# Layer A scores: the mask as 64 extra factors of queries and keys, in place of a mask product

## The chip, the cores and the metric

One core of a Trainium2 chip runs the whole program. TensorE multiplies, VectorE and ScalarE evict and transpose, GpSimd copies and issues small transfers, SyncE issues the streamed weights. The metric is the device time of one execution, in microseconds (us); lower is better. In the profile PE is TensorE's products, PEld its weight loads, DVE VectorE, ACT ScalarE, POOL GpSimd, SP SyncE.

## The reference, cut to what matters

Four layers in the order A, B, A, B, each added to its input after a layer norm. Only layer A is touched. It is a recurrence: the 2048 rows are cut into 64 segments of 32 rows, and eight memory rows that go in front of a segment are an output of the segment before it.

```python
L = M + seg_len                      # 8 + 32
mask = (idx[:, None] < M) | (idx[:, None] >= idx[None, :])
mem = mem0
for s in range(n_seg):               # 64 segments, one after the other
    h = concatenate([mem, xs], axis=1)
    q, k, v = einsum of h with Wq, Wk, Wv      # 32 heads of 192
    scores = einsum('bhqe,bhke->bhqk', q, k) * scale
    scores = where(mask, scores, -1e9)
    o = einsum('bhqk,bhke->bhqe', softmax(scores), v)
    o = einsum('bhte,hed->btd', o, Wo)
    mem = o[:, :M, :]
    outs.append(o[:, M:, :])
```

## The kernel before

**Tiling.** A segment's heads are worked in four rounds of eight. In one round the 32 rows that depend on the recurrence (8 memory rows and 24 rows of the segment) are projected on the chain; the last 8 rows of each segment don't depend on it as queries and keys, and a preparation stage (`A_pre`) has computed them for all segments and stored them in DRAM (`kqb_d`, `vb_d`). A score matrix is 80 by 80 for two heads: 2 x 32 columns of chain rows and 16 of prepared rows.

**Eight heads as six chunks.** The projection of queries (or keys) of one round gives 128 partitions by 384 columns in PSUM (`project`): six chunks of 64 columns. A head has 192 features, which is one chunk of 128 and a half. Three chunks hold two heads: chunk 0 is the one head's, chunk 2 the other's, and the middle chunk is shared, its upper 64 partitions one head's rest and its lower 64 the other's. `to_raw` evicts the 384 columns to bf16 (ScalarE), `to_rows` transposes them into `KT` or `QT` (VectorE). For the queries GpSimd then copies the second half of both middle chunks into two chunks of their own (line 1075) and clears it in its old place (line 1076), so that the half that belongs to the other head meets zeros.

**Scores.** `scores` opens the PSUM bank with a mask product: the identity (80 by 80) times a constant mask tile, four times side by side, 320 columns (line 1091). Six products add the scores (line 1098): four of 80 columns, two of 160. `weigh` takes the exponential (ScalarE, line 1181).

**A segment in program order.** `A_chain` is scheduled by hand: each engine runs its instructions in the order in which they are written. Round 0 projects Q, K and V. For n = 0, 1, 2 the steps are: project Q of round n + 1; scores and exponential of round n; `next_kq` puts prepared columns into `KT` and `QT` (GpSimd, line 1036); in round 1 sixteen products with Wo; project K of round n + 1; `attend` round n (lines 1111 and 1118); `tails_after`, a transfer issued by GpSimd that brings 16 prepared value rows into one of two value tiles (`extra_v`, line 1040), read two rounds later and issued when `attend` has read that tile; `fetch_kq` (line 1031); project V of round n + 1; weighing and transposing the outputs. After V of round 3 come the last scores, with steps of the output product around them: `STEPS` says how many ahead of the scores and how many between scores and `attend`. The segment ends with `attend` of round 3, the last twelve output steps, four filling products (`keep_busy`), and the new memory rows (`wt`, `hT`), which the next segment's first Q projection waits for.

**Streamed weights.** Not all weights fit. Per segment SyncE issues seven loads of 384 KB (three Wq, two Wk, two Wv slots, line 705) and four of 320 KB (`wo_rows`, line 750). Each waits for one step on TensorE: every projection releases one load when it is done (`self.release(last)`), in the order Wq, Wq, Wq, Wk, Wk, Wv, Wv, then the four Wo pieces. The Wv slots are read by V of round 3, the Wo pieces by the segment's last steps.

**Stores.** With s > 0, the tail output of the segment before is evicted after K of round 0, transposed and stored after V of round 0 (`store_tail`, line 1156); the rows of the segment before are stored after `fetch_kq` of round 0 (`store_rows`, line 1027). The transfers that GpSimd issues run in the order of its program.

Of the kernel before, what the change touches and what calls it, by code (L numbers as in the profile page):

```python
# [8 lines left out]
P = 128  # L9
BF16 = mybir.dt.bfloat16  # L10
F32 = mybir.dt.float32
# [16 lines left out]

STEPS = (1, 5)

# [4 lines left out]
def ap3(ap, dims):  # L35
    return bass.AP(tensor=ap.tensor, offset=ap.offset, ap=[list(d) for d in dims])
# [86 lines left out]
class Kernel:  # L123
# [508 lines left out]
    def build_A_consts(self):  # L632
        nc, const = self.nc, self.const

        mk = const.tile([P, 80], BF16, name="mask_st")
        nc.gpsimd.memset(mk[:], MASK_NEG)

        def keep(m, base, pattern, mult):  # L640
            nc.gpsimd.affine_select(out=m, in_=m, compare_op=ALU.is_ge, fill=MASK_NEG, base=base, pattern=pattern,
                                    channel_multiplier=mult)

        for G in range(2):
            for c in (slice(32 * G, 32 * G + 32), slice(64 + G, 80, 2)):
                nc.gpsimd.memset(mk[32 * G:32 * G + 32, c], 0.0)
            keep(mk[32 * G:32 * G + 32, 32 * G + 8:32 * G + 32], 8, [[1, 24]], -1)
            for c in (slice(32 * G, 32 * G + 8), slice(64 + G, 80, 2)):
                m = mk[64:80, c]
                nc.gpsimd.memset(m, 0.0)  # L650
                if G == 0:
                    keep(m, 7, [[0, 8]], -1)
                else:
                    keep(m, -8, [[0, 8]], 1)
                if c.start >= 64:
                    keep(m, 8 * G, [[1, 8]], -1)
        self.mk = mk

# [128 lines left out]
    def A_pre(self, xn_dram, li, load_matrix, piece, wo_mid, wo_end, lay_out_wo, early_wo, x_raw):  # L787
# [12 lines left out]
        with ExitStack() as es:  # L800
# [102 lines left out]
            for h, ri, r in steps:  # L903
# [14 lines left out]
                turn += 1  # L918
                if x_raw is not None and h == 0 and ri == 1:
                    self.build_A_consts()  # L920
# [56 lines left out]
    def A_chain(self, xn_dram, at_dram, li, load_slot, piece, late_wo, load_both, wo, low):  # L977
# [3 lines left out]
        with tc.tile_pool(name=f"A{li}_ch", reuse_waits="tile", bufs=1) as sp, \  # L981
                tc.tile_pool(name=f"A{li}_pq", reuse_waits="tile", bufs=2, space=bass.MemoryType.PSUM) as pqp, \
                tc.tile_pool(name=f"A{li}_po", reuse_waits="tile", bufs=1, space=bass.MemoryType.PSUM) as pop, \
                tc.manual_schedule():
            KT = sp.tile([P, 6, 80], BF16, name="KT")
            QT = sp.tile([P, 8, 80], BF16, name="QT")
            Vs = [sp.tile([P, 4 * VH], BF16, name=f"Vp{i}") for i in range(2)]
# [3 lines left out]
            ots = [self.under[:, self.ot_at + 384 * i:self.ot_at + 384 * i + 384] for i in range(2)]  # L991
            for i, t in enumerate((KT, QT, *Vs)):
                (nc.vector if i % 2 else nc.gpsimd).memset(t[:], 0.0 if i < 2 else 1.0)
            xv = xn_dram.rearrange("(s t) d -> t s d", t=32)
# [4 lines left out]
            def rounds(s):  # L999
                return range(NR) if s % 2 == 0 else range(NR - 1, -1, -1)  # L1000
# [33 lines left out]
            def extra_kq(kqb):  # L1034
                for t, c in ((QT, 96), (KT, 0)):
                    nc.gpsimd.tensor_copy(out=t[:, 0:6, 64:80], in_=kqb[:, c:c + 96].rearrange("p (c q) -> p c q", q=16))

# [4 lines left out]
            def project(hT, ps, m, n, s, steps):  # L1042
                order = rounds(s)
                r = order[n]
                ns = SLOTS[m]
                for i in steps:
                    b = (i + KC - ns) % KC if n == 0 else i
                    w = piece(m, r, b)
                    for g in range(4):
                        if m == "V":  # L1050
                            hp = 2 * (g % 2) + g // 2
                            rhs = w[:, 384 * hp:384 * hp + 384]
                        else:
                            w3 = w[:, 32 * g:32 * g + 32]
                            rhs = ap3(w3, [list(w3.ap[0]), [P, 6], [768, 2], [1, 32]])
                        o = ps
                        last = nc.tensor.matmul(o[32 * g:32 * g + 32, 0:384], lhsT=hT[:, b, :], rhs=rhs, start=(i == 0),  # L1057
                                         stop=(i == KC - 1), tile_position=(0, 32 * g), skip_group_check=True)
# [6 lines left out]

            def to_raw(ps, tag):
                raw = sp.tile([P, 384], BF16, name="raw", tag=tag)
                nc.scalar.activation(out=raw[:], in_=ps[:, 0:384], func=ACT.Copy)  # L1068
                return raw

            def to_rows(raw, m):
                t = KT if m == "K" else QT
                nc.vector.transpose(out=t[:, 0:6, 0:64], in_=raw[:, :].rearrange("p (c j) -> p c j", j=64))  # L1073
                if m == "Q":
                    nc.gpsimd.tensor_copy(out=QT[64:P, 6:8, :], in_=QT[64:P, 1:5:3, :])  # L1075
                    nc.gpsimd.memset(QT[64:P, 1:5:3, :], 0.0)  # L1076

# [9 lines left out]
            def scores():  # L1087

                S = pop.tile([P, 512], F32, name="ps_s", tag="s")
                m = self.mk[0:80, :]  # L1090
                nc.tensor.matmul(S[0:80, 0:320], lhsT=self.ident[0:80, 0:80], rhs=ap3(m, [list(m.ap[0]), [0, 4], [1, 80]]),  # L1091
                                 start=True, stop=False, skip_group_check=True)
                for x in range(2):
                    for i, q in ((0, slice(3 * x, 3 * x + 1)), (1, slice(3 * x + 1, 7 + x, 5 - 2 * x)),
                                 (2, slice(3 * x + 2, 3 * x + 3))):
                        c0 = 160 * x + (80 if i == 2 else 0)
                        n = 2 if i == 1 else 1
                        nc.tensor.matmul(S[0:80, c0:c0 + 80 * n], lhsT=KT[:, 3 * x + i, :], rhs=QT[:, q, :],  # L1098
                                         start=False, stop=(x == 1 and i == 2), skip_group_check=True)
                return S  # L1100
# [48 lines left out]

            def turn_tail(rows):  # L1150
                otb = sp.tile([P, 192], BF16, name="otb", tag="otb", bufs=2)
                self.chain_end = [nc.vector.transpose(out=otb[:], in_=rows[:])]  # L1152
                return otb

            def store_tail(otb, s, r):
                nc.gpsimd.dma_start(out=self.otb_d[:, s, 192 * (r // 2):192 * (r // 2) + 192], in_=otb[:])  # L1156

# [52 lines left out]
            for s in range(NSEG):  # L1210
# [3 lines left out]

                def q_or_k(m, n):
                    ps = pqp.tile([P, 512], F32, name="ps_qk", tag="qk")
                    project(hT, ps, m, n, s, range(KC))
                    return to_raw(ps, "rawk" if m == "K" else "raw")

# [14 lines left out]
                raw = q_or_k("K", 0)  # L1234
                to_rows(raw, "K")
                if s > 0:
                    rows = tail_rows(rct, "OTh")
                if s == 0:
# [3 lines left out]
                v_rows(pv, 0, "sv")  # L1242
                if s > 0:
                    store_tail(turn_tail(rows), s - 1, rounds(s - 1)[L])
                OTs = []
# [18 lines left out]
                for n in range(L):  # L1264
                    raw = q_or_k("Q", n + 1)
                    if n == 2:
                        otb = turn_tail(otr)
                    E = weigh()
                    next_kq(s, n)
                    to_rows(raw, "Q")  # L1270
                    if n == 1:
# [17 lines left out]
                    if n == 1:  # L1289
                        rct = weigh_tail()  # L1290
                    to_rows(raw, "K")
                    pv = v_banks()
# [36 lines left out]
                wo_round(W, order[L], OTs[L], False, True)  # L1329
                idle = pqp.tile([P, 512], F32, name="ps_idle", tag="qk")  # L1330
                for _ in range(4):
# [10 lines left out]
                W_done = W  # L1342
            store_tail(turn_tail(tail_rows(rct, "OTh")), NSEG - 1, order[L])
            keep_rows(W_done)
# [83 lines left out]
```

## Time and profile before

| | us |
|---|---|
| median of 3 runs | 3346.97 |
| lowest and highest | 3339.17, 3349.75 |
| the profiled execution, its own time | 3343.23 |
| span of its trace | 3341.5 |
| TensorE, VectorE, ScalarE, GpSimd busy | 3154.1, 2132.4, 1778.2, 1581.9 |
| the mask product, 512 times, mean of one | 0.331 |
| eviction of queries or keys, 1024 times, mean of one | 0.490 |
| transposition of queries, 512 times, mean of one | 0.579 |

A row of a group reads: line, engine, operation, output<-inputs, shape, count | busy time, mean of one in ns | idle time of the engine just before, and what ended it. A row of the timeline or of the chain of waits reads: start in us, length in us, engine, line, operation, xcount. Lengths of products include the pipeline, so the distance between two starts, not the length, is what a product takes from TensorE. A DMA row of the chain of waits runs from the issue to the landing that ended the wait.

### The profile page before, as it was taken

What the parts mean: (1) busy time and instruction counts of PE and PEld (TensorE: products, weight loads), DVE (VectorE), ACT (ScalarE), POOL (GpSimd) and SP (SyncE); (2) the same over time, 40 slices, a digit from 0 to 9 for tenths busy, and PEclk for the clock granted to TensorE, in tenths of its full rate; (3) what the DMA queues carried; (4) which work ended last, traced back from release to release, by engine and by line L of the source; (5) the groups of instructions that cost most, each with busy time, mean ns of one, the idle gap of its engine ahead of it and who ended that gap; (6) DMA issues with size and microseconds to landing.
All of it is one profiled execution on the core that took longest, in us unless ns stands there. A gap on an engine that the chain in (4) does not pass through costs nothing.

```text
span 3341.5 us, 141361 instructions
## 1 busy us (share of the span) xinstructions
PE 3154.1 (94%) x58946; PEld 2007.3 (60%) x59218; DVE 2132.4 (64%) x5569; ACT 1778.2 (53%) x4225; POOL 1581.9 (47%) x3921
## 2 busy tenths in 40 slices
PE   9889999999999999899999899999999999998999
PEld 7656666656666666555367566666666666665553
DVE  5456666666666666646643566666666666666565
ACT  3245555555555565546433455555555555655363
POOL 3345555555555555530123455555555555555300
PEclk9999999999999999999999999999999999999999
DMA  8887777767767777750285767777677776768400
GB/s 308 317 297 235 241 242 238 255 225 249 245 228 254 238 253 240 266 175 1 101 305 194 243 233 250 236 246 248 230 251 239 248 246 233 255 232 284 135 1 32
DMA packets 325241, 747.58 MB, mean 224 GB/s; under 512 B 66066, under 2 KB 100490, under 8 KB 321530
## 3 DMA queue, kind: packets, MB, share of 16 engines
q1 hardware_dynamic: 254586, 638.46, 54.7%
q0 software_dynamic: 67808, 86.77, 8.9%
q10 hardware_dynamic: 2208, 13.30, 1.0%
q8 instruction: 465, 7.62, 0.9%
q14 instruction: 174, 1.43, 0.1%
HBM read 668.78 MB, written 77.00 MB: 223 GB/s over the span
## 4 chain that ended last, share of the span: by engine, by line
PE 55%; DMA 19%; POOL 7%; DVE 6%; issue 5%; ACT 2%; POOLq 0%; SPq 0%; DVEq 0%; ACTq 0%
PE ps_qk L1057 15%; PE ps_w L1163 10%; DMA Vp<-vb 9%; PE ps_v L1057 6%; DMA arena<-in_A_Wv_dram 5%; DMA arena<-wo_rows 4%; PE ps_pre L936 3%; PE kv L1383 2%; DVE wt L1337 2%; PE ps_o L1111 2%; PE ps_s L1098 2%; PE ps_wo L429 2%; PE ps_s L1091 2%; PE ps_pre L963 2%; DVE hT L1339 2%
## 5 line engine op out<-in xcount | busy, mean ns | idle before, releaser
L1057 PE MATMUL ps_qk<-arena,hT 128*32 128x384 bf16 x20480 | 996.1, 327 | 51.9 <-DVE hT L1339 37.9
L1057 PEld LDWEIGHTS <-hT 128*32 128x32 bf16 x30720 | 785.6, 96 | 429.5 <-issue 39.1
L1068 ACT ACTIVATE raw<-ps_qk 128x384 bf16<-128x384 f32 x1024 | 502.0, 490 | 519.7 <-PE ps_qk L1057 515.4
L1057 PE MATMUL ps_v<-arena,hT 128*32 128x384 bf16 x8192 | 432.7, 326 | 10.8 <-DMA arena<-in_A_Wv_dram 9.3
L1136 ACT ACTIVATE osc<-ps_o,rc 128x192 bf16<-128x192 f32 x896 | 334.6, 417 | 140.0 <-DVE rc L1130 129.1
L1073 DVE STREAM_TRANSPOSE QT<-raw 128x384 bf16<-128x384 bf16 x512 | 296.3, 579 | 155.0 <-ACT raw L1068 99.3
L1075 POOL COPY QT<-QT 64x160 bf16<-64x160 bf16 x512 | 163.2, 319 | 487.9 <-DVE QT L1073 472.0
L1040 POOL DMA_DIRECT2D Vp<-vb x512 | 257.6, 503 | 202.1 <-issue 99.1
L1073 DVE STREAM_TRANSPOSE KT<-raw 128x384 bf16<-128x384 bf16 x512 | 295.9, 578 | 78.6 <-ACT raw L1068 62.5
L1085 DVE CAST Vp<-ps_v 64x384 bf16<-64x384 f32 x512 | 286.3, 559 | 50.6 <-ACT Vp L1083 38.5
L1163 PE MATMUL ps_w<-arena,under 128*32 128x320 bf16 x6144 | 304.7, 301 | 2.3 <-issue 1.9
L1031 POOL DMA_DIRECT2D kqb<-kqb x512 | 292.3, 571 | 18.9 <-DMA vb<-arena 1.8
L1083 ACT ACTIVATE Vp<-ps_v 64x384 bf16<-64x384 f32 x512 | 247.9, 484 | 16.6 <-PE ps_v L1057 13.9
L1181 ACT ACTIVATE E<-ps_s 80x320 bf16<-80x320 f32 x512 | 221.4, 432 | 59.4 <-PE ps_s L1098 42.1
L1020 ACT ACTIVATE wh<-ps_w 64x160 f32<-64x160 f32 x256 | 76.6, 299 | 309.8 <-DVE wt L1337 265.8
L1098 PE MATMUL ps_s<-QT,KT 128*80 128x80 bf16 (+1 forms) x3072 | 234.2, 213 | 7.2 <-POOL QT L1076 3.5
L1156 POOL DMA_DIRECT2D otb<-otb x256 | 142.2, 555 | 203.1 <-DVE otb L1152 202.8
L1126 DVE RECIPROCAL rc<-ps_o 128x2 f32<-128x2 f32 x384 | 65.5, 171 | 247.9 <-PE ps_o L1111 247.6
L1098 PEld LDWEIGHTS <-KT 128*80 128x80 bf16 x3072 | 209.9, 119 | 17.8 <-issue 4.2
L936 PEld LDWEIGHTS <-arena 128*128 128x128 bf16 x1920 | 189.1, 99 | 43.7 <-DMA arena<-in_A_Wk_dram 13.2
L1111 PE MATMUL ps_o<-Vp,E 80*32 80x193 bf16 x4096 | 178.7, 248 | 37.6 <-DMA Vp<-vb 31.9
L94 DVE CAST arena<-ps_pre 128x512 bf16<-128x512 f32 (+1 forms) x160 | 102.3, 646 | 144.3 <-PE ps_pre L936 97.1
(161 smaller groups left out, 5115.2 us busy)
## 6 DMA issues: line engine op xcount, KB each, us to landing
arena<-wo_rows SPq DMA_DIRECT2D x560, 320.0 KB, 6.2
arena<-in_A_Wq_dram SPq DMA_DIRECT2D x427, 384.0 KB, 3.8
arena<-in_A_Wk_dram SPq DMA_DIRECT2D x298, 384.0 KB, 5.1
arena<-in_A_Wv_dram SPq DMA_DIRECT2D x290, 384.0 KB, 6.0
kqb<-kqb POOLq DMA_DIRECT2D x512, 48.0 KB, 4.6
vb<-arena POOLq DMA_DIRECT2D x128, 97.0 KB, 5.9
Vp<-vb POOLq DMA_DIRECT2D x512, 24.2 KB, 4.6
kqb<-arena SPq DMA_DIRECT2D x8, 1536.0 KB
```

Source lines behind the costliest of these rows:

```text
L936: nc.tensor.matmul(ps[:, T * i:T * i + T], lhsT=w[b][:, P * c:P * c + P], rhs=xBT[:, b, :], start=(b == 0), stop=(b == KC - 1))
L1031: nc.gpsimd.dma_start(out=kqb[:], in_=self.kqb_d[r, :, s, :])
L1040: nc.gpsimd.dma_start(out=Vs[n % 2][64:80, :], in_=self.vb_d[s, r].rearrange("g t f -> (g t) f"))
L1057: last = nc.tensor.matmul(o[32 * g:32 * g + 32, 0:384], lhsT=hT[:, b, :], rhs=rhs, start=(i == 0), stop=(i == KC - 1), tile_position=(0, 3 ...
L1068: nc.scalar.activation(out=raw[:], in_=ps[:, 0:384], func=ACT.Copy)
L1073: nc.vector.transpose(out=t[:, 0:6, 0:64], in_=raw[:, :].rearrange("p (c j) -> p c j", j=64))
L1083: nc.scalar.activation(out=o, in_=i, func=ACT.Copy)
L1085: nc.vector.tensor_copy(out=o, in_=i)
L1098: nc.tensor.matmul(S[0:80, c0:c0 + 80 * n], lhsT=KT[:, 3 * x + i, :], rhs=QT[:, q, :], start=False, stop=(x == 1 and i == 2), skip_group_c ...
L1111: nc.tensor.matmul(O[G][32 * h:32 * h + 32, VH * G:VH * G + 193], lhsT=E[0:80, 80 * h + 32 * G:80 * h + 32 * G + 32], rhs=V[0:80, VH * h:V ...
L1136: nc.scalar.activation(out=out, in_=i, func=ACT.Copy, scale=rc[G])
L1163: step = nc.tensor.matmul(W[q:q + 32, 0:320], lhsT=OT[i // 6][:, i % 6 // 2, 32 * (i % 2):32 * (i % 2) + 32], rhs=rhs, start=(first and i ...
```

## The change

The middle chunk is now two chunks, each with one half occupied: a round's queries (and keys) take 8 chunks, 512 columns, four for each pair of heads. `project` writes the 384 columns into a PSUM bank with a gap: partitions 0 to 63 leave chunk 3 of each four empty, partitions 64 to 127 chunk 0. Queries and keys have one PSUM bank each, kept for the whole layer (`psq`, `psk`), and the empty halves of these banks hold 64 constant factors, written once per layer: `w` with the queries and `u` with the keys, built so that their product is the mask. Evicting and transposing 512 columns carries them along; the columns of the prepared rows have factors of their own (`wt`, `ut`), written once into `KT` and `QT`. So the mask product goes, the scores become eight products of 80 columns, and the two GpSimd steps on the queries' halves go.

With it come these moves:

- Eviction (ScalarE) and transposition (VectorE) of queries and keys have 512 columns in place of 384. Keys of round 3 are done in two halves of 256.
- The prepared columns go into `KT` and `QT` (now one tile `QK`) with two copies of 64 partitions by 192 elements in place of two of 128 by 96.
- The tail of the segment before is evicted, transposed and stored, and its rows are stored, ahead of the first Q projection's eviction. The rows' store comes first.
- `STEPS` is (2, 5) in place of (1, 5).
- The transposed tails lie in parts of `ots` instead of tiles of their own; the bank for the filling products is the one of the scores.
- The factors are built by GpSimd in the preparation stage of both A layers (24 instructions; the mask tile was built once), and eight small VectorE copies at the start of each chain place them.

```diff
-STEPS = (1, 5)
+STEPS = (2, 5)
...
+            QK = sp.tile([P, 2, 8, 80], BF16, name="QK")
+            KT, QT = QK[:, 0], QK[:, 1]
+            psq, psk = [pqp.tile([P, 512], F32, name=f"ps_qk_{m}") for m in "qk"]
...
+            u, w, ut, wt = self.factors()
+            for ps, part, t, tail in ((psq, w, QT, wt), (psk, u, KT, ut)):
+                for h, c in ((slice(64, P), 0), (slice(0, 64), 3)):
+                    o = ps[h, :].rearrange("p (x c j) -> p x c j", c=4, j=64)[:, :, c, :]
+                    nc.vector.tensor_copy(out=o, in_=bcast_mid(part[h, :], 2))
+                    nc.vector.tensor_copy(out=t[h, c:8:4, 64:80], in_=bcast_mid(tail[h, :], 2))
...
-                for t, c in ((QT, 96), (KT, 0)):
-                    nc.gpsimd.tensor_copy(out=t[:, 0:6, 64:80], in_=kqb[:, c:c + 96].rearrange("p (c q) -> p c q", q=16))
+                for b in range(2):
+                    h = slice(64 * b, 64 * b + 64)
+                    o = QK[h].rearrange("p m (x c) j -> p (m x) c j", x=2)[:, :, b:b + 3, 64:80]
+                    nc.gpsimd.tensor_copy(out=o, in_=kqb[h, :].rearrange("p (x c q) -> p x c q", c=3, q=16))
...
+                        if m != "V":
+                            o = ps[32 * g:32 * g + 32, :].rearrange("p (x c) -> p x c", x=2)[:, :, 64 * (g // 2):64 * (g // 2) + 192]
...
-                    nc.gpsimd.tensor_copy(out=QT[64:P, 6:8, :], in_=QT[64:P, 1:5:3, :])
-                    nc.gpsimd.memset(QT[64:P, 1:5:3, :], 0.0)
...
-                nc.tensor.matmul(S[0:80, 0:320], lhsT=self.ident[0:80, 0:80], rhs=ap3(m, [list(m.ap[0]), [0, 4], [1, 80]]),
-                                 start=True, stop=False, skip_group_check=True)
...
+                    for c in range(4):
+                        c0 = 160 * x + 80 * (c // 2)
+                        nc.tensor.matmul(S[0:80, c0:c0 + 80], lhsT=KT[:, 4 * x + c, :], rhs=QT[:, 4 * x + c, :],
+                                         start=(c % 2 == 0), stop=(c % 2 == 1), skip_group_check=True)
...
                 if s > 0:
                     keep_rows(W_done)
-                to_rows(q_or_k("Q", 0), "Q")
+                    rows = tail_rows(rct, "OTh")
+                    otb = turn_tail(rows, ots[1][:, 0:192])
+                    store_rows(s - 1)
+                    store_tail(otb, s - 1, rounds(s - 1)[L])
+                turn_rows(q_or_k("Q", 0))
...
-                    raw = q_or_k("K", n + 1)
+                    raw = q_or_k("K", n + 1, n + 1 == L)
...
-                    if n == 0 and s > 0:
-                        store_rows(s - 1)
```

More of the change, by code (lines that the diff above doesn't have):

```diff
@@ L632, in build_A_consts @@
     def build_A_consts(self):
[L633 to L642, printed above, removed]
-        for G in range(2):
[L645 to L656, printed above, removed]
@@ L659, in layer_A, with factors @@
+        for t in (u, w, ut, wt):
+            nc.gpsimd.tensor_copy(out=t[64:P, :], in_=t[0:64, :])
+    def factors(self):
+        at, out = self.ot_at + 768, []
+        for n in (64, 64, 16, 16):
+            out.append(self.under[:, at:at + n])
+            at += n
+        return out
     def layer_A(self, xn_dram, at_dram, li, x_raw=None):
@@ L918, in A_pre @@
                 turn += 1
-                if x_raw is not None and h == 0 and ri == 1:
+                if h == 0 and ri == 1:
                     self.build_A_consts()
@@ L1064, in values, with to_rows, turn_rows @@
                 project(hT, pv, "V", n, s, steps)
[L1066 to L1071, printed above, removed]
-                t = KT if m == "K" else QT
[L1073 to L1076, printed above, removed]
+            def to_rows(ps, m, halves=False):
+                t = KT if m == "K" else QT
+                raw = sp.tile([P, 512], BF16, name="raw", tag="rawk" if m == "K" else "raw")
+                cols = (slice(0, 256), slice(256, 512)) if halves else (slice(0, 512),)
+                for c in cols:
+                    nc.scalar.activation(out=raw[:, c], in_=ps[:, c], func=ACT.Copy)
+                return [(t[:, c.start // 64:c.stop // 64, 0:64], raw[:, c].rearrange("p (c j) -> p c j", j=64)) for c in cols]
+            def turn_rows(pairs):
+                for o, i in pairs:
+                    nc.vector.transpose(out=o, in_=i)
             def v_rows(pv, n, engines):
@@ L1213, in A_chain, with q_or_k @@
                 L = NR - 1
-                def q_or_k(m, n):
-                    ps = pqp.tile([P, 512], F32, name="ps_qk", tag="qk")
+                def q_or_k(m, n, halves=False):
+                    ps = psk if m == "K" else psq
                     project(hT, ps, m, n, s, range(KC))
-                    return to_raw(ps, "rawk" if m == "K" else "raw")
+                    return to_rows(ps, m, halves)
                 def v_banks():
@@ L1290, in A_chain @@
                         rct = weigh_tail()
-                    to_rows(raw, "K")
+                    turn_rows(raw)
                     pv = v_banks()
```

59 lines of the change are left out of this document (30 added, 29 removed).

## The prediction

> **What bounds the kernel now.** I read the page first, then the chain of waits in order of time over some segments, the timeline of one of them, and the busy times by stretch.
>
> ```profile
> PE 3154.1 (94%) x58946; PEld 2007.3 (60%) x59218; DVE 2132.4 (64%) x5569; ACT 1778.2 (53%) x4225; POOL 1581.9 (47%) x3921
> PE 55%; DMA 19%; POOL 7%; DVE 6%; issue 5%; ACT 2%; POOLq 0%; SPq 0%; DVEq 0%; ACTq 0%
> PE ps_qk L1057 15%; PE ps_w L1163 10%; DMA Vp<-vb 9%; PE ps_v L1057 6%; DMA arena<-in_A_Wv_dram 5%; DMA arena<-wo_rows 4%; PE ps_pre L936 3%; PE kv L1383 2%; DVE wt L1337 2%; PE ps_o L1111 2%; PE ps_s L1098 2%; PE ps_wo L429 2%; PE ps_s L1091 2%; PE ps_pre L963 2%; DVE hT L1339 2%
> ```
>
> TensorE is busy 94% of the span, but only 55% of the chain is its own: 18 of the 19% of DMA are three transfers of layer A's chain. In order of time:
>
> ```profile
> 1004.95 6.45 DMA arena<-in_A_Wv_dram
> ...
> 1027.67 6.61 DMA arena<-wo_rows
> ...
> 1035.78 1.02 PE ps_qk L1057 x20
> ...
> 1043.22 0.67 POOL attn L1027
> ...
> 1044.52 0.32 POOL QT L1075
> ...
> 1044.92 0.20 POOL QT L1076
> 1045.12 0.31 issue
> 1045.43 5.28 DMA Vp<-vb
> ...
> 1054.47 1.81 PE ps_qk L1057 x40
> ```
>
> The first rows are from two segments, the others from a third, 1054.47 - 1035.78 = 18.69 us long. One ended on the second Wv slot, one on the last Wo piece, the third on the prepared value rows, whose transfer was issued late because GpSimd was busy with the rows' store and the two steps on the queries' halves. From the shares and these lengths I estimate how many of the 128 segments end on each: Vp 9% of 3341 / 5.28 = 57, Wv 5% / 6.45 = 26, Wo 4% / 6.61 = 20, and some 25 on none of them. So in four of five segments, work taken from TensorE ahead of the wait turns into a longer wait. The question is what moves the landings.
>
> ```profile
> 1017.00:1018.00 1.00, 1.00 (x28) 0.67 (x32) 0.61 (x3) 0.43 (x3) 0.00 (x0) 1.00 0.14 36
> 1018.00:1019.00 1.00, 1.00 (x32) 0.67 (x28) 0.53 (x2) 0.68 (x2) 0.00 (x0) 1.00 0.11 15
> 1019.00:1020.00 1.00, 1.00 (x32) 0.65 (x24) 0.73 (x2) 0.99 (x3) 0.55 (x2) 1.00 0.82 227
> 1021.00:1024.00 3.00, 3.00 (x78) 1.99 (x71) 2.21 (x5) 2.16 (x6) 2.29 (x7) 1.00 0.94 343
> 1024.00:1029.00 5.00, 5.00 (x125) 3.39 (x126) 3.62 (x10) 3.47 (x9) 3.60 (x10) 1.00 1.00 338
> 1032.00:1035.80 3.80, 3.23 (x72) 1.84 (x63) 2.32 (x10) 0.82 (x3) 1.93 (x4) 1.00 0.29 86
> arena<-wo_rows SPq DMA_DIRECT2D x560, 320.0 KB, 6.2
> arena<-in_A_Wq_dram SPq DMA_DIRECT2D x427, 384.0 KB, 3.8
> arena<-in_A_Wk_dram SPq DMA_DIRECT2D x298, 384.0 KB, 5.1
> arena<-in_A_Wv_dram SPq DMA_DIRECT2D x290, 384.0 KB, 6.0
> attn<-under POOLq DMA_DIRECT2D x128, 40.0 KB, 6.0
> xr<-xn POOLq DMA_DIRECT2D x126, 40.0 KB, 2.7
> ```
>
> The last two columns of the stretches are the DMA engines' busy share and GB/s, over one segment. The engines idle at its two ends (0.14, 0.11, 0.29) and are full in between. In the order of their issue the weights take 3.8, 5.1, 6.0 and 6.2 us to land: a backlog grows. A store of 40 KB issued into it takes 6.0 us (attn), a load of 40 KB at the segment's end 2.7 (xr). Small transfers queue with the weights.
>
> **The change part by part.**
>
> *Scores.*
>
> ```profile
> 1042.50 0.33 PE L1091 MATMUL ps_s<-mask_st,ident 80*80 80x320 bf16 x1
> 1042.62 0.49 ACT L1068 ACTIVATE raw<-ps_qk 128x384 bf16<-128x384 f32 x1 [0.33 <-PE ps_qk L1057]
> 1042.67 0.45 PE L1098 MATMUL ps_s<-QT,KT 128*80 128x80 bf16 x6
> 1043.05 0.73 PE L1163 MATMUL ps_w<-arena,under 128*32 128x320 bf16 x16
> 1043.16 0.43 ACT L1181 ACTIVATE E<-ps_s 80x320 bf16<-80x320 f32 x1
> ...
> 1043.61 0.98 PE L1057 MATMUL ps_qk<-arena,hT 128*32 128x384 bf16 x20
> ```
>
> Start to start, the mask product takes 0.17 us and the six others 0.38 (640 columns). Afterwards the mask's 0.17 is gone and eight products move the same 640 columns. Two more starts cost between nothing (columns decide) and 2 x 0.06 (0.38 / 6 each); I take nothing: the mask's 320 columns take 0.53 ns each and the 640 of six products 0.59, so columns decide. So a round saves 0.17 (0.05 to 0.17). Three of the four rounds lie ahead of the segment's landings: 0.51. In the last, `STEPS` puts one more output step, four products, ahead of the scores; 16 of them take 1043.61 - 1043.05 = 0.56, so four take 0.14 and the last exponential comes 0.03 earlier.
>
> [...]
>
> *Wider evictions and transpositions.*
>
> ```profile
> L1068 ACT ACTIVATE raw<-ps_qk 128x384 bf16<-128x384 f32 x1024 | 502.0, 490 | 519.7 <-PE ps_qk L1057 515.4
> L483 ACT ACTIVATE arena<-ps_pq 120x512 bf16<-120x512 f32 x80 | 42.6, 601 | 23.4 <-PE ps_pq L480 22.9
> L1073 DVE STREAM_TRANSPOSE QT<-raw 128x384 bf16<-128x384 bf16 x512 | 296.3, 579 | 155.0 <-ACT raw L1068 99.3
> L1262 DVE STREAM_TRANSPOSE under<-osc 128x192 bf16<-128x192 bf16 x256 | 76.3, 336 | 0.1
> ```
>
> An eviction of 512 columns takes 0.60 us (L483), 0.11 more; a transposition by the slope of the last two rows 0.579 + 128 x 1.27 ns = 0.74, 0.16 more. Both engines have room, so the place that counts is the exponential: it follows the Q eviction on ScalarE, and `attend` waits for it. Relative to the scores' start it runs from 0.12 + 0.60 = 0.72 to 1.15. `attend` can start when the scores (0.38) and K's projection (20 products, 0.79 by 1.81 for 40 against 1.02 for 20) are through, at 1.17. It hides with 0.02 to spare. Without that cover it would cost 0.1 in two rounds, 0.2 us of a segment that isn't waiting for a transfer: 5 us over 25 of them.
>
> *GpSimd.*
>
> ```profile
> L1075 POOL COPY QT<-QT 64x160 bf16<-64x160 bf16 x512 | 163.2, 319 | 487.9 <-DVE QT L1073 472.0
> L1036 POOL COPY KT<-kqb 128x96 bf16<-128x96 bf16 x512 | 133.3, 260 | 0.1
> 1044.59 0.26 PE L1118 MATMUL ps_t<-Vp,E 80*16 80x193 bf16 x4
> ...
> 1051.01 0.27 PE L1118 MATMUL ps_t<-Vp,E 80*16 80x193 bf16 x4
> ...
> 1051.58 0.51 POOL L1040 DMA_DIRECT2D Vp<-vb  x1 [0.59 <-PE ps_t L1118]
> ```
>
> Per round a copy (0.32) and a clearing (0.23) go; the two prepared copies grow from 0.26 to about 0.35 each (slope 0.92 ns per element from the two rows). In round 3, where GpSimd waits for `attend`, the value transfer is issued 0.30 us after the last product's end (1051.58 less 1051.01 + 0.27); in round 1 0.58 (1045.43 less 1044.59 + 0.26). With the clearing and the rows' store out of the way it comes at 0.30, 0.28 earlier; two mask products ahead of it add 0.34: issued 0.62 earlier. If it takes 5.28 as now, it lands 0.62 earlier. If it lands in its place in the backlog, it gains only what the backlog loses.
>
> [...] The 6.0 against 2.7 above speak for something nearer to a queue.
>
> *Moved stores.*
>
> ```profile
> q0 software_dynamic: 67808, 86.77, 8.9%
> ```
>
> The small transfers take 8.9% of the span for 86.77 MB, 3.4 us per MB. The rows' store (40 KB) and one tail store (48 KB) leave the full stretch for the segment's start, where the engines idle: between nothing and 0.31 us (0.09 MB x 3.4) off the backlog that the value rows and the Wo pieces stand in; I take most of it, 0.25. Only the rows' store comes newly ahead of the Wv slots; they move by -0.15 to +0.15. On GpSimd these two issues now precede the first prepared copies, which wait for the scores of round 0 anyway; ahead of the first Q eviction ScalarE gets one 0.4 us step while Q is still being projected (1.02 us).
>
> *The sum, by what a segment ends on.* Vp: the landing comes between 0.25 and 0.62 earlier, then the last Wo piece binds. I take 0.45: 57 x 0.45 = 25.7 us. Wo: the backlog's 0.25 and a little: 20 x 0.3 = 6. Wv: 26 x 0.15 = 3.9. The others: 3 x 0.17 + 0.03 = 0.54 until a landing binds; I take 0.35: 25 x 0.35 = 8.8. Together 44. Building the factors a second time, 24 short GpSimd steps (some 0.25 each, 6 us) while it idles in the preparation, and eight small copies: 0 to 6, I take 2. The profiled execution took 3343.2, so 3301; the median of the runs is 3.7 above it, so 3305.
>
> **The rivals.**
>
> *The waits take it back.* Every landing keeps its place, and only the 25 free segments gain, by 0.2 before a landing binds: 3347 - 5 = 3342. For it: DMA 0.94 to 1.00 busy for 8 us of a segment. Against it: two stores leave that stretch.
>
> *Everything comes forward.* Weight loads, released up to 0.34 earlier, and value rows land as much earlier, and no landing binds before the 0.54 are in: 126 x 0.54 = 68, with the relief of the value rows up to 85: 3275. For it: the engines idle at the segments' ends. Against it: 6.2 us to land means a backlog.
>
> *Slower.* The rows' store, now ahead of all weights of its segment, delays the second Wv slot, while V of round 3 wants it 0.51 earlier, so twice as many segments, 50, wait there. At 0.3 us of delay (its issue alone takes 0.67) less the 0.03 won after, 50 x 0.27 = 13: 3360. It decides from the point where the delay exceeds the backlog's relief. The exponential's lost cover would be another 5.
>
> **How the numbers follow.** About 0.3%, 10 us, is what a measurement tells from no change. The forecast (20 to 65 faster) has 0.51, everything forward 0.16, taken back 0.15, slower 0.18. Faster by over 0.3%: 0.51 + 0.16 + 0.01 = 0.68; within: 0.14; slower: 0.18. The range goes from beyond the second rival, 3265, to half way into the slower one, 3353; the forecast's own is 3282 to 3327.
>
> **What would show it.** Right: the scores' 0.55 us become 0.38; the value transfer of round 1 is issued 0.3 us after `attend`; Vp's share of the chain falls to a few per cent while Wv's and Wo's rise; segments of 18.4 to 18.6 us. Wrong: Vp still near 9%; waits for Wv grown past 0.5 us a segment; `attend` waiting for the exponential in rounds 0 and 2; DVE or ACT at the head of the chain.

## The result, and the profile after

The changed kernel takes 3307.0 us (median of 4 runs, 3299.36 to 3309.9) against 3343.07 for the kernel before (median of 4, 3337.86 to 3349.75). The ratio is 0.9887, 95% interval 0.986 to 0.9915: 36 us less, where 42 were forecast. The profiled execution took 3309.6 with a span of 3307.9, against 3343.2 and 3341.5 before.

The page of the changed kernel: busy times, the chain by engine and by line, and the row of the instruction queue, which will matter.

```profile
PE 3097.4 (94%) x59424; PEld 1976.7 (60%) x59730; DVE 2265.7 (68%) x5711; ACT 1837.0 (56%) x4353; POOL 1423.4 (43%) x2926
PE 70%; DMA 13%; DVE 10%; issue 4%; ACT 2%; POOL 1%; SPq 0%; PEld 0%; ACTq 0%; DVEq 0%; POOLq 0%
PE ps_qk_q L1073 12%; PE ps_qk_k L1073 11%; PE ps_v L1073 10%; PE ps_w L1173 10%; DMA arena<-in_A_Wv_dram 6%; PE ps_s L1109 5%; PE ps_pre L941 4%; DMA Vp<-vb 4%; PE ps_o L1122 2%; DVE wt L1344 2%; PE kv L1390 2%; PE ps_pre L968 2%; PE ps_wo L429 2%; DVE hT L1346 2%; PE ps_pq L480 1%
...
q8 instruction: 469, 7.68, 1.0%
```

TensorE's share of the chain has risen from 55 to 70% and the transfers' has fallen from 19 to 13%: value rows from 9 to 4%, Wv from 5 to 6, Wo from 4 to below the list. One round's scores in the timeline of the changed kernel, and GpSimd's issue of the value rows in round 1:

```profile
1006.24 0.26 PE L1129 MATMUL ps_t<-Vp,E 80*16 80x193 bf16 x4
1006.81 0.50 POOL L1054 DMA_DIRECT2D Vp<-vb  x1 [1.26 <-PE ps_t L1129]
...
1019.91 0.50 PE L1109 MATMUL ps_s<-QK 128*80 128x80 bf16 x8
1020.03 0.60 ACT L1087 ACTIVATE raw<-ps_qk_q 128x512 bf16<-128x512 f32 x1 [0.33 <-PE ps_qk_q L1073]
1020.34 0.83 PE L1073 MATMUL ps_qk_k<-arena,hT 128*32 128x384 bf16 x16
1020.53 0.42 ACT L1191 ACTIVATE E<-ps_s 80x320 bf16<-80x320 f32 x1
1020.66 0.71 DVE L1092 STREAM_TRANSPOSE QK<-raw 128x512 bf16<-128x512 bf16 x1 [0.32 <-ACT raw L1087]
```

Eight score products take 1020.34 - 1019.91 = 0.43 us from start to start, where 0.55 stood before. The value rows are issued 1006.81 - (1006.24 + 0.26) = 0.31 us after `attend`, and GpSimd now waits for TensorE there, here 1.26 us. The issues by line, median us to landing last:

```profile
arena<-wo_rows SPq DMA_DIRECT2D x560, 320.0 KB, 6.0
arena<-in_A_Wq_dram SPq DMA_DIRECT2D x427, 384.0 KB, 4.2
arena<-in_A_Wk_dram SPq DMA_DIRECT2D x298, 384.0 KB, 5.3
arena<-in_A_Wv_dram SPq DMA_DIRECT2D x290, 384.0 KB, 5.5
...
attn<-under POOLq DMA_DIRECT2D x128, 40.0 KB, 3.7
```

The rows' store now lands in 3.7 us, not 6.0; a Wv slot in 5.5, not 6.0; a Wo piece in 6.0, not 6.2. What TensorE waited for (total us, times, longest), before:

```profile
PE ps_o L1111 <- DMA Vp<-vb: 31.9, 61, 1.6
PE ps_w L1163 <- issue: 9.7, 18, 1.1
PE ps_v L1057 <- DMA arena<-in_A_Wv_dram: 9.3, 22, 1.1
```

and after:

```profile
PE ps_w L1173 <- issue: 36.8, 48, 1.7
PE ps_v L1073 <- DMA arena<-in_A_Wv_dram: 14.2, 33, 0.9
PE ps_o L1122 <- DMA Vp<-vb: 9.6, 23, 1.2
```

The waits for value rows have fallen by 22 us. But the output products (`ps_w`) now stand 36.8 us in "issue", in gaps of up to 1.7 us that no semaphore ends. So the question for the experiments is twofold: which part of the change won the 36 us, and what these gaps are.

### The profile page after: what moved, and what is told of

Read it like the earlier page. It is cut to its first block, busy times and chain, and to the rows that moved or that the text cites. A ratio compares the mean times of both kernels' runs of the same rounds, so it can differ in the third digit from the quotient of the medians.

```text
span 3307.9 us, 141147 instructions
## 1 busy us (share of the span) xinstructions
PE 3097.4 (94%) x59424; PEld 1976.7 (60%) x59730; DVE 2265.7 (68%) x5711; ACT 1837.0 (56%) x4353; POOL 1423.4 (43%) x2926
## 4 chain that ended last, share of the span: by engine, by line
PE 70%; DMA 13%; DVE 10%; issue 4%; ACT 2%; POOL 1%; SPq 0%; PEld 0%; ACTq 0%; DVEq 0%; POOLq 0%
PE ps_qk_q L1073 12%; PE ps_qk_k L1073 11%; PE ps_v L1073 10%; PE ps_w L1173 10%; DMA arena<-in_A_Wv_dram 6%; PE ps_s L1109 5%; PE ps_pre L941 4%; DMA Vp<-vb 4%; PE ps_o L1122 2%; DVE wt L1344 2%; PE kv L1390 2%; PE ps_pre L968 2%; PE ps_wo L429 2%; DVE hT L1346 2%; PE ps_pq L480 1%
## 5 line engine op out<-in xcount | busy, mean ns | idle before, releaser
L1092 DVE STREAM_TRANSPOSE QK<-raw 128x512 bf16<-128x512 bf16 (+1 forms) x1152 | 730.4, 643 | 214.8 <-ACT raw L1087 159.1
L1073 PE MATMUL ps_qk_q<-arena,hT 128*32 128x384 bf16 x10240 | 509.6, 327 | 57.0 <-DVE hT L1346 38.6
L1050 POOL COPY QK<-kqb 64x192 bf16<-64x192 bf16 x1024 | 349.9, 342 | 395.3 <-PE ps_s L1109 357.5
L1073 PE MATMUL ps_qk_k<-arena,hT 128*32 128x384 bf16 x10240 | 511.9, 329 | 3.2 <-ACT raw L1087 1.0
L1087 ACT ACTIVATE raw<-ps_qk_k 128x512 bf16<-128x512 f32 (+1 forms) x640 | 313.6, 511 | 257.6 <-PE ps_qk_k L1073 257.5
L1073 PE MATMUL ps_v<-arena,hT 128*32 128x384 bf16 x8192 | 438.0, 327 | 16.7 <-DMA arena<-in_A_Wv_dram 14.2
L1087 ACT ACTIVATE raw<-ps_qk_q 128x512 bf16<-128x512 f32 x512 | 305.7, 597 | 165.4 <-PE ps_qk_q L1073 150.7
L1101 DVE CAST Vp<-ps_v 64x384 bf16<-64x384 f32 x512 | 286.2, 559 | 35.3 <-ACT Vp L1099 20.4
L1109 PEld LDWEIGHTS <-QK 128*80 128x80 bf16 x4096 | 195.8, 121 | 159.4 <-issue 157.9
L1109 PE MATMUL ps_s<-QK 128*80 128x80 bf16 x4096 | 256.4, 210 | 3.4 <-issue 3.1
L1039 POOL DMA_DIRECT2D attn<-under x128 | 91.9, 718 | 324.3 <-DVE under L1035 321.1
```

What stands on the lines that cost most here:

```text
L1050: nc.gpsimd.tensor_copy(out=o, in_=kqb[h, :].rearrange("p (x c q) -> p x c q", c=3, q=16))
L1073: last = nc.tensor.matmul(o, lhsT=hT[:, b, :], rhs=rhs, start=(i == 0), stop=(i == KC - 1), tile_position=(0, 32 * g), skip_group_check=True)
L1087: nc.scalar.activation(out=raw[:, c], in_=ps[:, c], func=ACT.Copy)
L1092: nc.vector.transpose(out=o, in_=i)
L1101: nc.vector.tensor_copy(out=o, in_=i)
L1109: nc.tensor.matmul(S[0:80, c0:c0 + 80], lhsT=KT[:, 4 * x + c, :], rhs=QT[:, 4 * x + c, :], start=(c % 2 == 0), stop=(c % 2 == 1), skip_gro ...
```

## The gaps

Such a gap in the changed kernel's chain:

```profile
1028.60 0.64 PE ps_v L1073 x14
1029.24 0.55 issue
1029.79 0.48 PE ps_v L1073 x5
```

TensorE stops for 0.55 us in the middle of a projection and waits for nothing that the profile shows. The instruction queue (q8) fetches 469 packets of 16 KB, one for every 256 of TensorE's some 120,000 recorded instructions. I took all places where two products start over 0.2 us apart, no semaphore ends the gap, and its end lies 1.1 to 1.7 us behind the end of such a fetch; the length of a gap is that distance less 0.045 us and comes out longer than the idle time in the rows above. In the kernel before, all 32 of them that are over 0.3 us long stand at the same place of every 256 instructions (the 193rd to 195th, by the count of recorded instructions); in the changed kernel 74 of 76 do (193rd or 194th in the first chain, 175th or 176th in the second, between which some records are missing). Nothing in the program has a period of 256; a segment has 840 recorded instructions before and 848 after. So I take them for waits for the next block of instructions; no row of the profile names them so. Of the 127 and 116 shorter ones only 17 each stand near that place, so the sums below hold some 20 us that are not such waits (the same count finds 23.0 and 24.0 us in the two runs with half transfers further down).

```
gaps behind instruction fetches, us (number)    all          of these in the output products
before                                          43.7 (159)   17.0 (29)
changed                                         90.8 (192)   51.0 (56)

fetch starts in the segment at (us)           0-4    4-8    8-11   11-16
and this long after its lead begins (us)      0.7    2.8    3.4    3.6    (median, changed kernel)
```

No fetch of the two kernels starts more than some 290 instructions ahead of that place; its lead is counted from 288 ahead, which is 5.7 to 6.0 us of TensorE's time. At the segment's start it begins 0.7 us later; in the full stretch 3.6 us later, takes 1.05 (median of the 469 packets), and behind the gaps of over 0.3 us TensorE goes on some 1.4 after its end: 3.6 + 1.05 + 1.4 = 6.05. There the lead is used up. Of the 76 gaps of over 0.3 us all but one lie behind the segment's twelfth microsecond. Whether the wait costs time, or only fills time that a landing would have taken, the next section tells.

## Experiments

"Expected" is what stood on record before the run. Ratios are to the kernel before on the same chip.

**Stores put back.** The changed kernel with the old places of the rows' store and of the tail store.

```diff
@@ start of a segment
-                    rows = tail_rows(rct, "OTh")
-                    otb = turn_tail(rows, ots[1][:, 0:192])
-                    store_rows(s - 1)
-                    store_tail(otb, s - 1, rounds(s - 1)[L])
@@ behind V of round 0
+                if s > 0:
+                    store_tail(turn_tail(rows, ots[1][:, 0:192]), s - 1, rounds(s - 1)[L])
@@ behind fetch_kq of round 0
+                    if n == 0 and s > 0:
+                        store_rows(s - 1)
```

> The changed kernel with its two moved stores put back into the rounds (rows' store behind attend of round 0, tail store behind V of round 0); the rest as changed. Theory L (landings): the rows and the tail take 88 KB, some 0.25 us, of the full stretch again; the Wo pieces and the value rows of round 3 land 0.2 to 0.3 us later, the segments that end on a landing or on an instruction fetch grow by as much: 15 to 25 us over the changed kernel's 3307, so 3322 to 3332. Theory P (TensorE's own time is what was won): stores don't touch TensorE, 3307 to 3312.

Measured 0.9967 (0.9953 to 0.998), 3332 by 3343: at the upper end of what theory L expected. All of the change but the moved stores wins 11 us.

**Stores alone.** The kernel before with the same two stores moved to the segment's start, nothing else.

> The kernel before with nothing but the two stores moved to the segment's start; mask product, copies of halves, narrow evictions and STEPS as before. Theory L: the value rows' issue of round 1 comes earlier by what the rows' store held GpSimd (0.28 us) and everything in the full stretch lands 0.2 to 0.25 earlier: 15 to 25 us under the kernel before, ratio 0.9925 to 0.9955. Theory P: ratio 0.998 to 1.000.

Measured 0.9893 (0.9877 to 0.9908): 36 us, more than either theory gave, and not to be told from the whole change. Its page and its waits:

```profile
PE 71%; DMA 15%; DVE 6%; issue 3%; PEld 2%; ACT 2%; POOL 1%; SPq 0%; DVEq 0%; POOLq 0%; ACTq 0%
...
PE ps_o L1111 <- DMA Vp<-vb: 14.4, 28, 1.1
PE ps_v L1057 <- DMA arena<-in_A_Wv_dram: 13.9, 27, 1.3
...
L1163 PE MATMUL ps_w<-arena,under 128*32 128x320 bf16 x6144 | 303.7, 301 | 2.2 <-DMA arena<-wo_rows 2.0
```

TensorE is busy 3144.6 us here and 3097.4 in the changed kernel, and both end together: 47 us of products taken away, with all that came in their place, won nothing. Where they went is seen from the means over 126 segments (124 for the next segment's start), counted from the segment's first product:

```
us from the segment's first Q product   before  stores alone  changed  stores back
last weight of Wo lands                 17.07   16.78         16.57    17.05
value rows of round 3: issued            9.66    9.38          9.14     9.15
                       landed           14.99   14.67         14.49    14.62
scores of round 0 done                   3.91    3.91          3.79     3.79
scores of round 2 done                  11.17   11.18         10.82    10.83
attend of round 3 starts                15.22   15.06         14.84    15.05
filling products at the end start       17.86   17.64         17.62    17.80
next segment's first product            19.00   18.77         18.77    18.97
gaps behind fetches, all segments, us    43.7    35.3          90.8     89.8
```

Against stores alone, the changed kernel is 0.36 ahead after the scores of round 2, 0.22 at the last `attend`, and even with it at the end. Most of what it loses on the way is in the gaps: 51.0 us in the output products against 11.8, which is 0.31 a segment.

**Product back.** The changed kernel with a product of the mask product's size.

```diff
+                f = self.factors()[0][0:80, :]
+                nc.tensor.matmul(S[0:80, 0:320], lhsT=self.ident[0:80, 0:80], rhs=ap3(f, [list(f.ap[0]), [0, 5], [1, 64]]),
+                                 start=True, stop=True, skip_group_check=True)
```

> The changed kernel with one product of 80x80 on 320 columns ahead of the scores in each round, as the mask product was; its result is overwritten by the scores, so the output is the same. It costs TensorE 0.12 us a round, 0.48 a segment. Theory L: it costs 0.36 us in the some 74 segments that end on no landing, and less in the others, and a slower TensorE waits less for instruction fetches: 5 to 27 us, 3312 to 3334. Theory P: 126 x 0.48 = 60 us, 3360 to 3370. If nothing of it counts: 3307.

Measured 0.9949 (0.9932 to 0.9967), 3326: some 20 us for 0.14 a round (the scores with it take 0.57), within what theory L expected; theory P is out. So the product's absence is worth some 20 us in the changed kernel. But with the product this kernel is 17 us slower than stores alone, whose scores take nearly as long (0.55): by this difference the rest of the rebuilding costs about what the product's absence wins, and the half transfers show two parts of that cost where no transfer is waited for. The gaps shrink from 90.8 to 66.9 us (read from the longest of its six executions, 3337.7): a slower TensorE waits less for instructions here. Stores alone has 35.3, though, so a faster TensorE is not all that makes the gaps grow; what else does is open.

**Half transfers.** Both kernels with half of each streamed weight (`self.light` holds in the segments 1 to 61 of each layer's 64, here and in the next experiment, not 1 to 125 as the expectations say; the Wo pieces are cut likewise).

```diff
+                n = PW // 2 if self.light else PW
-                self.last_load = nc.sync.dma_start(out=slot[m, b], in_=wview[m][:, b, PW * r:PW * r + PW])
+                self.last_load = nc.sync.dma_start(out=slot[m, b][:, 0:n], in_=wview[m][:, b, PW * r:PW * r + n])
```

> The kernel before; in the segments 1 to 125 of each layer's chain each streamed weight transfer brings only the first half of its columns (the products use what lay in the other half, so the output isn't the reference's). Instructions and their order stay. Theory F (landings, and instruction fetches that stand in the same backlog): landings no longer bind, the gaps of TensorE in the output steps that end 1.1 to 1.7 us after an instruction fetch go from 17 us to under 5, and a segment takes about what the fastest twentieth takes now, 18.47 us: 126 x 0.53 = 67 us less, 3280. Theory P (TensorE's own time): under 20 us less.

> The changed kernel with the same half transfers. Theory F: the gaps behind instruction fetches in the output steps go from 51 us to under 5, no landing binds, and a segment takes the 18.02 us of the fastest twentieth: 3307 - 126 x 0.74 = 3213, so some 60 us under the kernel before with half transfers, which is the 0.48 us a segment that the mask product took. If the gaps have nothing to do with the backlog they stay near 50 us and the two kernels with half transfers lie 20 to 40 us apart.

Measured 0.9762 (0.9743 to 0.9781) and 0.9644 (0.9621 to 0.9666): 80 and 119 us less than the kernel before, 40 apart; theory F had expected 67 for the first and 60 between the two. Of the changed kernel with half transfers:

```profile
arena<-wo_rows SPq DMA_DIRECT2D x488, 160.0 KB, 3.2
arena<-in_A_Wv_dram SPq DMA_DIRECT2D x244, 192.0 KB, 3.0
...
L1176 PE MATMUL ps_w<-arena,under 128*32 128x320 bf16 x6144 | 302.9, 301 | 0.3 <-issue 0.3
L1176 PEld LDWEIGHTS <-QK 128*32 128x32 bf16 x3072 | 70.3, 96 | 91.7 <-DVE QK L1275 55.6 <-issue 21.4
```

and of the kernel before with them:

```profile
L1166 PEld LDWEIGHTS <-KT 128*32 128x32 bf16 x3072 | 70.4, 96 | 75.2 <-DVE KT L1266 38.3 <-issue 22.2
```

The gaps in the output products are gone (51.0 to 0.5 us, and 17.0 to 0): they do hang on the backlog of transfers, and fetches now start 1.4 us after their lead begins. With no such wait the change is worth 0.28 us a segment (18.31 against 18.03), not the 0.50 that its scores save (the last scores end 0.36 earlier, with one more output step of 0.14 ahead of them). The last two rows tell one reason: the last Wo steps wait for the last turned rows, 38.3 us before and 55.6 after. `STEPS` (2, 5) takes one output step from behind the last `attend` and puts it ahead of the last scores, and behind `attend` it had covered that way, 17 us over 126 segments. The rest, 0.08 a segment, lies ahead of the last `attend`. In both of these kernels that `attend` starts 0.05 us behind the end of VectorE's cast of the last values, in 98% of the segments; VectorE turns to this cast right after transposing outputs, and begins it only 0.27 us earlier than in the kernel before (13.77 against 14.04 us of the segment).

**Weights not waited for.** The changed kernel with all its transfers, but no product reads a streamed slot.

```diff
             assert (m, r, b) in res or holds[m, b] == r
+            if self.light and (m, r, b) not in res:
+                return res[m, 2, b]
...
-                        rhs = wo[r, i].rearrange("p (a g f) -> p a g f", a=2, g=2)[:, :, g, :]
+                        rhs = wo[1 if self.light and r in (0, 3) and i >= OWN else r, i].rearrange("p (a g f) -> p a g f", a=2, g=2)[:, :, g, :]
```

> The changed kernel; in the segments 1 to 125 of each layer's chain all weight transfers run as before, with all their bytes, but the products that would read a streamed slot read a resident piece of the same shape instead (so the output isn't the reference's). No product waits for a weight's landing; the backlog of transfers stays, and with it what stands in it: value rows and instruction fetches. Theory F (instruction fetches hold TensorE in their own right): the gaps behind fetches in the output steps stay at 40 to 70 us and the kernel ends between the 3218 of half transfers and 3307, at 3255 to 3290. Theory L (only landings do, the gaps merely fill time in which TensorE would wait for a landing anyway): 3215 to 3235.

Measured 0.9886 (0.9868 to 0.9905): no faster than the changed kernel at all, which neither theory had. Its waits and a transfer:

```profile
PE ps_w L1176 <- issue: 30.0, 46, 1.7
PE ps_o L1125 <- DMA Vp<-vb: 15.2, 30, 1.4
...
arena<-wo_rows SPq DMA_DIRECT2D x560, 320.0 KB, 6.1
```

The weights' landings, the wait that the prediction argued from, no longer set the time of the changed kernel by themselves. Against its half transfers this kernel takes 18.68 - 18.03 = 0.65 us more a segment, 82 us over 126; the gaps behind fetches hold 90.3 - 24.0 = 66 of them and the value rows 15.2 - 0.8 = 14. So four fifths of what the backlog still costs comes by way of the instruction fetches. That is a sum of rows; no run takes the fetches away and leaves the value rows.

**Fewer transfers under way.** To have fewer weights on their way when a fetch starts, each load also waits for the third (or second) load before it.

```diff
+                if len(under_way) == 3:
+                    tc.add_manual_dep(new.ins, under_way.pop(0).ins.name, data, reason="and fewer")
+                under_way.append(new)
```

> The changed kernel; each streamed weight transfer also waits until the third one before it has landed, so at most three stand in the queues. Bytes and order stay. Theory F: a weight lands every 1.0 to 1.5 us, so what stands ahead of an instruction fetch or a small transfer shrinks from some 5 us to some 3; the fetch gaps in the output steps fall from 51 us to 10 to 25, value rows land up to 1 us earlier: 20 to 40 us faster, 3267 to 3287. Rival: the wait itself opens holes in the transfers, the weights land later and the segments end on them: 3310 to 3360.

> The same with two. Theory F: the fetch gaps are all but gone, under 8 us; but a transfer alone needs some 3 us from issue to landing, two under way bring one each 1.5 us, so weights land about as fast as now or later by up to 2 us at the last Wo piece: 3270 if they keep up, 3340 or more if not.

Measured 1.0878 (1.0833 to 1.0923) and 1.271 (1.2677 to 1.2743): the rival, by far. Three and two under way:

```profile
SPq L710 <- DMA arena<-in_A_Wq_dram: 461.8, 391, 4.6
...
arena<-wo_rows SPq DMA_DIRECT2D x560, 320.0 KB, 4.4
```

```profile
arena<-wo_rows SPq DMA_DIRECT2D x560, 320.0 KB, 3.5
```

Landings get quicker, from 6.0 to 4.4 and 3.5 us, but not in proportion to the number under way; none was run alone. Three in 4.4 us are at best one each 1.5, 16 us for a segment's eleven, and with three SyncE stands 461.8 us in waits for Wq landings at one line (the row above), while the loads behind it in its program wait too. With three the gaps in the output products are gone, for TensorE waits elsewhere.

**Smaller parts.** GpSimd's steps back in their place; the third store of a segment moved to its end; `STEPS` at (1, 5) and (0, 5).

```diff
@@ GpSimd's steps
+                    for c in (QT[64:P, 1:3, :], QT[64:P, 5, :]):
+                        nc.gpsimd.tensor_copy(out=c, in_=c)
@@ third store: from behind attend of round 2 to behind load_rows
+                store_tail(otb, s, order[1])
@@ STEPS
-STEPS = (2, 5)
+STEPS = (1, 5)
```

> The changed kernel with two GpSimd copies of a part of the turned queries onto itself behind each turned Q of the rounds 1 to 3 (64 rows, 160 and 80 elements, 0.3 and 0.25 us), where the kernel before had its copy and its clearing; values are unchanged. GpSimd is 0.55 us busier ahead of the value transfer of a round. Theory L: the value rows of round 3 are issued 0.2 to 0.3 us later and land 0.1 to 0.3 later: 22 segments that wait for them and as many that then do, 5 to 12 us slower, 3312 to 3319. If the order of landings in the backlog decides, not the issue: 3305 to 3309.

> The changed kernel with the third store of the segment (the tails of round 1, 48 KB, issued behind attend of round 2) moved to the segment's end, behind the load of the next rows. Theory L: another 48 KB, 0.16 us, leave the full stretch: 5 to 12 us faster, 3295 to 3302. Rival: that store lies behind the transfers that decide, and at the segment's end it now stands ahead of the next segment's first weights: 3305 to 3315.

> The changed kernel with STEPS back at (1, 5): one output step, four products, less ahead of the last scores, and so one more behind the last attend, where it covers the way of the last rows from TensorE over ScalarE or VectorE back to TensorE. With half transfers that cover was 0.15 us a segment short in the changed kernel. Theory C (cover): the last scores come 0.14 earlier, the wait for the last turned rows falls by as much; segments that don't wait for value rows or Wo pieces, some 70, gain 0.14: 5 to 12 us faster, 3295 to 3302. Theory L alone (a landing takes it back everywhere): 3305 to 3309.

> The same with (0, 5): no output step ahead of the last scores. Theory C: another 0.14 of cover, but attend of the last round then starts some 0.28 earlier than in the changed kernel, at 14.57 us of the segment, against value rows that land at 14.49 on average: two thirds of the segments wait for them, and little comes on top: 3292 to 3302. If fetches decide: the output steps lie closer together behind attend, the gaps grow: 3305 to 3315.

Measured 0.989 (0.9875 to 0.9904), 0.9899 (0.9883 to 0.9914), 0.9878 (0.9863 to 0.9893) and 0.9879 (0.9859 to 0.9899): none can be told from the changed kernel's 0.9887. GpSimd's steps moved round 0's issue by 0.20 us and round 1's not at all (9.15), since GpSimd waits for `attend` there longer than the steps take (1.26 us in the row above). With (1, 5) the wait for the last turned rows falls, from 44.1 to 28.8 us, as its theory had it, and attend's wait for value rows rises:

```profile
L1173 PEld LDWEIGHTS <-QK 128*32 128x32 bf16 x3072 | 74.7, 96 | 79.7 <-issue 34.8 <-DVE QK L1271 28.8
...
PE ps_o L1122 <- DMA Vp<-vb: 14.6, 27, 1.1
```

A gain at one place of the last third is taken by the next wait. No kernel that moves all its bytes beats the changed one by more than its interval.

## Why the prediction was right, and where it was wrong

The time (3307 against 3305) was right, and so was the frame: what TensorE no longer does becomes a longer wait, and what moves the transfers decides. By its steps:

- *Scores.* 0.12 us a round, not 0.17: "I take nothing" for two more starts was wrong, eight products take 0.43 and not 0.38. The bounds (0.05 to 0.17) held. For each of these products of 80 columns, with its weight load, 0.43 is 54 ns.
- *Evictions and transpositions.* 0.60 us as forecast, and 0.71 for 0.74. `attend` of the rounds 0 and 2 didn't come to wait for the exponential.
- *GpSimd.* A copy takes 0.34 (forecast 0.35). The value rows of round 1 are issued 0.52 earlier, not 0.62: 0.28 from GpSimd, as forecast, and 0.24 from two mask products at 0.12. But the 0.28 does not need both moves: stores alone has it with the clearing and the copy in place (9.38), and the changed kernel issues at 9.15 with the rows' store put back and also with GpSimd's steps put back. Either of the two fits into GpSimd's wait for `attend`; only both together held the issue up. These rows land 5.35 us after their issue (14.49 less 9.14), 5.33 before: the landing moved with the issue, and did not keep its place in the backlog.
- *Moved stores.* This is the term that failed in size. I gave it 0.25 of relief inside a sum to which every part contributed. Alone it brings the last landings 0.29 to 0.32 forward (17.07 to 16.78, 14.99 to 14.67), about the upper bound of 0.31, though 0.28 of the value rows' 0.32 is their earlier issue. In the changed kernel, where the issue stays, it is 0.48 for the last Wo piece and 0.13 for the value rows (17.05 to 16.57, 14.62 to 14.49). And alone it wins 36 us, as much as the whole change.
- *The sum.* Its total fitted in part by luck, because two errors met. Too little went to the stores, and the shorter TensorE path was counted as a gain of its own (0.17 a round, in "the others" and in the earlier issue), while the rebuilding as a whole is worth 11 us without the moved stores and 2, less than can be told from nothing, with them. Its largest term held: the value rows land 0.50 earlier (0.45 taken), and TensorE's wait for them fell by 22 us (25.7). But the wait for Wv rose from 9.3 to 14.2 us, where a gain of 3.9 stood.
- *What was missed.* The prediction knew one thing that waits in the backlog, landings. Instruction fetches start later there too: 3.6 us after their lead begins in the full stretch, 1.4 with half the bytes. The gaps behind them hold 21 us before and 67 after (43.7 and 90.8, less the 23.0 and 24.0 of the runs with half transfers), and so take back most of what the shorter TensorE path wins; that is read from sums of rows, and what besides that path makes them grow is open. Of the rivals, "the waits take it back" was right for the rebuilding, by a wait that it hadn't named.
- *The signs.* Value rows at 4% of the chain and their issue 0.3 after `attend`: as forecast. Wv rose only to 6%, Wo fell instead of rising, and the median segment is 18.69 us, above the 18.4 to 18.6 forecast. The slower rival's delay of the Wv slots didn't come: the second lands at 12.60, 0.30 earlier.
- *Left open.* The 0 to 6 us for building the factors twice were not measured by themselves.

## What to carry to other kernels

Where transfers set the pace, look first for small ones that stand in the full stretch and could stand where the engines idle: two stores moved by a few lines won 36 us here, as much as the whole change. Before counting a shorter TensorE path as a gain, list everything that the same transfers hold up, the instruction stream too: its mark here was gaps of up to 1.7 us that no semaphore ends, in the middle of a group of products, at one place of every 256 recorded instructions. And a row of parts that each win when put on alone doesn't add up; undo them one at a time.

## What the runs showed of the hardware

- In the changed kernel an instruction fetch of 16 KB starts 0.7 us after its lead begins in the segment's first 4 us, where the transfer engines are 0.48 busy (mean over 124 segments), 2.8 and 3.4 us after it from 4 to 11 us, at 1.00 and 0.99, and 3.6 us after it from 11 to 16, at 0.83; with half the bytes of the weights 1.4. The fetches have a row of their own among the queues (q8, 1.0%). In what way the weights' transfers hold them up no run shows.
- A weight transfer stayed long with few under way: 384 or 320 KB land in 5.3 to 6.0 us in the full stretch, 3.5 to 4.1 with at most two under way, and half the bytes in 3.0 to 3.2. Throttling to two made the kernel 27% slower.
- In the two throttled kernels the mean granted clock of TensorE was lower, 0.965 with three under way and 0.901 with two, against 0.989 in the changed kernel. TensorE was busy 88 and 81% of the span there, against 94%: of these three, the one that waited more was also granted less.
